# Linear attention and two MLP layers on one core: operations pinned in their queues, key maxima and scalings in fewer or other VectorE operations, one conversion unit moved

## The chip, the cores and the metric

The kernel runs on one core of a Trainium2 chip. The metric is the device time in microseconds, the median of several runs. Before the change it is 864.81 us (three runs, 862.97 to 866.43).

## The reference, cut to what matters

```python
q_s = exp(q - max(q, axis=-1)); q_s = q_s / (sum(q_s, axis=-1) + 1e-9)
k_s = exp(k - max(k, axis=2));  k_s = k_s / (sum(k_s, axis=2) + 1e-9)
kv = einsum('bhsd,bhse->bhde', k_s, v)
x = einsum('bhsd,bhde->bhse', q_s, kv)       # then heads side by side: 2304 tokens x 512
h = x @ w_in;  r = maximum(h, 0);  x = (s * r*r + b) @ w_out          # 512 -> 2048 -> 512
h = x @ w2_in; x = (h * tanh(softplus(h))) @ w2_out                   # 512 -> 2048 -> 512
```

There are 4 batches of 8 heads with 576 positions of 64. The weights of both layers arrive in float64, of which the kernel makes float32 bit by bit.

## The kernel before, in words

**Numbers.** A float32 value is held as a high part `hi`, rounded by a ScalarE copy to the type fp32r, and a low part `lo`, the VectorE subtraction `src - hi` (`split` L169, `minus` L166). A product is then three matmuls, hi by hi, hi by lo, lo by hi (`passes` L173). In chunk 0 the first nine h steps and the first seven y steps use whole float32 operands instead.

**Tiling.** The 2304 tokens are cut into five chunks, 512, 256, 512, 512 and 512 (chunks 0 to 4), and the 2048 hidden columns into 16 blocks. A *step* is one chunk and one block, so there are 80 steps; chunk c starts at step 16 c. At step n the main loop (L943) emits the y product of step n and, two steps ahead, the h product of step n + 2 with its relu and square. After step 78 the second layer begins for pairs of chunks by a seven-product scheme with operands P1 to P7 (`h_unit`, `y_pair`).

**What else runs between the products.** `at(step, kind, fn)` enters a function for a step, and `run` calls what is due; the place in the loop depends on the kind ("early", "bits", "unit", "load" and so on).

- *Weights of the first layer* (L146, L158). Pair j of weight blocks (for j = 0 w_in blocks 0 and 1, else w_in block j + 1 and w_out block j - 1) is loaded (`load_w`), converted by `bits` (a ScalarE absolute value, L129, then four VectorE operations, L130 to L141, on 128 x 1024 elements) at step j - 3, and split at step j - 2 for j of 8 and more, at step 12 + j for the others.
- *Attention of the chunks from 1 on*, a pair of heads hp at a time, in stages: `att1` (key maximum over the rows L712, transposed on TensorE and reduced; q maximum L724 and subtraction L725), `att2` (key shift L736, q exponential L740), `att3` (key exponential, q sum, reciprocal, scaling L759), `att4_mm` (kv product, q transpose), `att4`, `att5`, `att5_mm` (x). For chunk c of 2 and more, `att1` of pair hp stands at step 16 (c - 1) + 3 hp - 1, for chunk 1 at step 2 hp + 3. Chunk 0's attention runs before the loop, with its q subtraction and q scaling on POOL. `x_split` (L195) splits x two steps ahead of the next chunk.
- *Weights of the second layer*: 32 units (`unit_load`, `unit_sums`, `unit_split`): a load, `bits` on 128 x 512 elements, four sums of 128 x 128, two splits of 128 x 512, two stores from POOL's queue. STARTS (L186) gives the half step of each: three in chunk 1, 29 in chunks 2 to 4.
- *Operands of the second layer*, in chunk 4 (L0 is step 64): `b_load` reads chunks 0 and 2 back, `b_next` makes one of seven operands for each of two halves kb (`put_slot` L375), into the weight slots `w0` to `w6` as the y products of chunk 4 leave them. `ring_load` (L409) fetches second-layer weights from POOL's queue into the slots of RING (L395), first at steps L0 + 9, 11 and 13.

**What sets the order of the instructions.** Each engine executes one queue in order. A scheduler fills these queues at build time: by a model of the run, it takes an instruction when its inputs are ready, so work can stand in a queue ahead of work that the program emits earlier. `pin` (L289) ties an instruction behind all that the program has emitted before it on that engine. Pinned before the change are the relus from step U1 on, ScalarE's share of the units, and the second-layer loads on POOL.

Of the kernel before, what the change touches and what calls it, by code (L numbers as in the profile page):

```python
# [31 lines left out]
def kernel(  # L32
# [113 lines left out]
    def conv_bits(j):  # L146

        if j < WHOLE:
            t = wp.tile([P, 4 * DM], F32, tag=f"w{j}", name=f"t{j}")[:, 0:2 * DM]
        else:  # L150
            t = cv.tile([P, 2 * DM], F32, tag=f"t{j % 2}", name=f"t{j}")
        t = t.rearrange("p (z f) -> p z f", z=2)
        w_t[j] = t
        for i, (z, f) in enumerate(members(j)):
            W[z, f] = (None, t[:, i])
        bits(t, w_raw.pop(j))

# [7 lines left out]

    def minus(eng, lo, src, hi):  # L166
        eng.tensor_tensor(out=lo, in0=src, in1=hi.bitcast(F32), op=ALU.subtract)  # L167

    def split(hi, lo, src, eng=None, pin=lambda ins: None):  # L169
        pin(nc.scalar.copy(out=hi, in_=src))  # L170
        minus(eng or nc.vector, lo, src, hi)

# [11 lines left out]
    U0 = 2 * NF  # L184
    U1 = U0 - 9
    STARTS = [2 * U1, 2 * U1 + 6, 2 * U1 + 12] + [2 * U0 + 2 * (NS - 2 - U0) * e // 29 for e in range(29)]  # L186
    x_t, x_next, x_whole = {}, {}, {}
# [101 lines left out]
    def pin(ins):  # L289
        tc.keep_in_program_order(ins)  # L290
# [83 lines left out]
    def put_slot(r, kb, src):  # L374
        if kb == 0:  # L375
            x_op[r] = wp.tile([P, 2, 2, CM], F32R, tag=f"w{Y_ORDER.index(r)}", name=f"xo{r}")
        split(x_op[r][:, 0, kb], x_op[r][:, 1, kb], src)

# [13 lines left out]
    for pair in range(len(PAIRS)):  # L392
        ring += [("wi", F, i) for F in range(NU) for i in range(2)]
        ring += [("wo", r, i) for r in Y_ORDER for i in range(2)]
    RING = ("ws0", "last", "ws1")  # L395
    ring_t, ring_free, ring_done, ring_out = {}, list(RING), [], [None]
# [300 lines left out]
    def att1(b, c, hp):  # L697

        if b is not None:
# [6 lines left out]
            else:  # L706
# [4 lines left out]

            nc.vector.tensor_reduce(  # L712
                out=km.rearrange("p (h d o) -> p h d o", h=2, o=1),
                in_=kb.rearrange("p h r d -> p h d r"), axis=AX.X, op=ALU.max,
            )
            ps = att_ps(b == 0, hp % 2, f"km{b}_{hp}")
# [6 lines left out]
        mx = ap.tile([P, 2 * CM // P, 1], F32, tag="qm", name=f"qm{c}_{hp}")[:, 0:2 * rq, :]  # L723
        nc.vector.tensor_reduce(out=mx, in_=t, axis=AX.X, op=ALU.max)  # L724
        (nc.vector if c else nc.gpsimd).tensor_tensor(  # L725
# [3 lines left out]
    def att2(b, c, hp):  # L729
        if b is not None:  # L730
            kb = kv_in[b, hp][0]
            ps, km, ke = kv_mid[b, hp]
            nc.tensor.matmul(out=ps, lhsT=ones, rhs=km, start=True, stop=True)
            km = ps.rearrange("p (h d) -> p h d", h=2)
            for h in range(2):
                nc.vector.tensor_tensor(  # L736
                    out=ke[:, :, h, :], in0=kb[:, h], in1=km[:, h:h + 1, :].to_broadcast([P, RK, D]),
                    op=ALU.subtract,
                )
        nc.scalar.activation(out=q_in[c, hp], in_=q_in[c, hp], func=AF.Exp)  # L740

    def att3(b, c, hp):
# [13 lines left out]
        qn = qn[:, 0:2 * rq * D].rearrange("p (r h d) -> p r h d", r=rq, h=2)  # L756
        for h in range(2):
            o = slice(h * rq, (h + 1) * rq)
            (nc.vector if c else nc.gpsimd).tensor_tensor(  # L759
                out=qn[:, :, h, :], in0=t[:, o, :], in1=sm[:, o, :].to_broadcast([P, rq, D]), op=ALU.mult  # L760
            )
        q_in[c, hp] = qn
# [27 lines left out]

    def kv_hi(b, hp):
        hi = ap.tile([P, P], F32R, tag="kvh", bufs=NP + 1, name=f"kvh{b}_{hp}")
        lo = ap.tile([P, P], F32R, tag="kvl", bufs=NP + 1, name=f"kvl{b}_{hp}")
        kv_t[b, hp] = (hi, lo)
        nc.scalar.copy(out=hi, in_=bds[hp if b == 0 else NP])

    def kv_lo(b, hp):
        minus(nc.vector, kv_t[b, hp][1], bds[hp if b == 0 else NP], kv_t[b, hp][0])

# [64 lines left out]
    for c in range(1, NC):  # L864
        wide = CHUNKS[c - 1] == CM
        for hp in range(NP):
# [11 lines left out]
            if c == 1:  # L878
                at(hp, "att1", kv_hi, 0, hp)
                at(hp, "att1", kv_lo, 0, hp)  # L880
            at(s + o[1], "att2", att2, b, c, hp)
# [10 lines left out]
    L0 = (NC - 1) * NF  # L892
    at(U1 - 3, "load", unit_load, 0)
    for e, i in enumerate(STARTS):
# [48 lines left out]
    for n in range(NS):  # L943
# [121 lines left out]
```

## Time and profile before

| what | value |
|---|---|
| median of three runs | 864.81 us (862.97 to 866.43) |
| the profiled execution | 868.49 us |
| its span, first to last instruction | 866.7 us |
| mean granted TensorE clock | 0.988 of full speed |
| TensorE busy with matmuls | 828.4 us (96%) |
| VectorE, ScalarE, POOL busy | 616.9 us (71%), 440.8 us (51%), 109.3 us (13%) |

A matmul's busy time is modelled from its pipeline, so TensorE at 100% of a stretch says that no gap is seen, not that it runs at its peak. "Idle before" is the time an engine stood still before an instruction, and its releaser is what ended the wait. PEclk is the share of full clock that was granted.

### The profile page before, as it was taken

Reading aid. Unit: us, or ns where it says so; the run is one execution under the profiler, and the core shown is the slowest. Engines: PE = TensorE matmul, PEld = TensorE weight load, DVE = VectorE, ACT = ScalarE, POOL = GpSimd, SP = SyncE. Lnnn points to the kernel's source line nnn. Section 1 sums busy time; section 2 is a strip of 40 time slices with the busy share of each in tenths; the row PEclk is TensorE's granted clock in tenths of the full one; section 3 lists DMA queues with packets and bytes.
Section 4 is the critical chain, followed back from the end, with each engine's and each line's share of the span. In section 5 each row is a group of like instructions: output and inputs, shape, how many; then the busy total and the mean of one; then the engine's idle time right before and its main releaser. Section 6 shows DMA issues by size and latency. Waiting matters only on the chain.

```text
span 866.7 us, 11570 instructions
## 1 busy us (share of the span) xinstructions
PE 828.4 (96%) x4084; PEld 666.0 (77%) x4084; DVE 616.9 (71%) x1153; ACT 440.8 (51%) x786; POOL 109.3 (13%) x196
## 2 busy tenths in 40 slices
PE   3799999998999999999989999989999999999998
PEld 2344787987888888888868878868788888878897
DVE  6989997568888887766887448687864655786511
ACT  3645777547666666555765435255442333544322
POOL 4000000000011001120212211101111111112110
PEclk9899999998999999999999999999999999999999
DMA  6994123144666556456656889657678866687891
GB/s 170 311 376 143 27 66 112 54 103 149 207 199 205 191 196 220 165 182 216 217 186 202 272 244 374 201 189 242 220 233 281 250 177 223 217 280 262 255 375 68
DMA packets 90474, 179.02 MB, mean 207 GB/s; under 512 B 26928, under 2 KB 45104, under 8 KB 86832
## 3 DMA queue, kind: packets, MB, share of 16 engines
q0 software_dynamic: 30256, 112.73, 40.0%
q1 hardware_dynamic: 59072, 64.50, 24.2%
q10 hardware_dynamic: 1088, 1.05, 0.4%
q8 instruction: 32, 0.52, 0.3%
q14 instruction: 26, 0.21, 0.1%
HBM read 131.60 MB, written 46.66 MB: 206 GB/s over the span
## 4 chain that ended last, share of the span: by engine, by line
PE 69%; DVE 13%; DMA 11%; SPq 2%; issue 2%; ACT 2%; POOL 0%; DVEq 0%; ACTq 0%; POOLq 0%
PE P L177 22%; PE h L177 16%; PE y L177 16%; PE rh L177 3%; PE ry L177 3%; DMA q<-in_q_dram 2%; DMA raw<-in_moe_w_out_dram 2%; DVE g L348 2%; DMA kb<-in_k_dram 2%; DVE w L167 1%; DVE gly_P L167 1%; PE P3y L177 1%; PE P5y L177 1%; PE P7y L177 1%; PE P4y L177 1%
## 5 line engine op out<-in xcount | busy, mean ns | idle before, releaser
L177 PE MATMUL h<-xh,w 128*128 128x512 f32 (+1 forms) x568 | 177.6, 378 | 7.8 <-ACT r L240 4.2
L177 PE MATMUL y<-gh,w 128*128 128x512 f32 (+1 forms) x584 | 176.6, 369 | 0.0
L177 PE MATMUL P<-xoP,rw 128*128 128x512 f32 x672 | 155.2, 390 | 1.0 <-DMA rw<-wdi 1.0
L177 PEld LDWEIGHTS P<-xoP,rw 128*128 128x128 f32 x672 | 125.8, 188 | 27.3 <-issue 1.4
L177 PEld LDWEIGHTS h<-xh,w 128*128 128x128 f32 x568 | 106.2, 194 | 26.6 <-ACT r L240 4.9
L177 PEld LDWEIGHTS y<-gh,w 128*128 128x128 f32 x584 | 106.5, 188 | 17.8
L170 ACT CAST ghy_P<-g 128x512 fp32r<-128x512 f32 x112 | 69.7, 623 | 82.4 <-DVE gly_P L167 34.7
L455 DVE TENSOR_TENSOR s<-s,P 128x512 f32<-128x512 f32 x112 | 75.2, 684 | 47.7 <-PE P L177 38.3
L177 PE MATMUL h<-xl,w 128*128 128x512 f32 (+1 forms) x284 | 106.7, 376 | 0.4 <-DVE xl L167 0.4
L177 PE MATMUL y<-gl,w 128*128 128x512 f32 (+1 forms) x292 | 106.8, 369 | 0.0
L167 DVE TENSOR_TENSOR gly_P<-g,ghy_P 128x512 fp32r<-128x512 f32 x112 | 75.8, 688 | 40.1 <-ACT ghy_P L170 39.2
L177 PE MATMUL P<-ghy_P,rw 128*128 128x512 f32 x224 | 87.2, 391 | 0.0
L458 ACT ACTIVATE g<-s 128x512 f32<-128x512 f32 x64 | 39.9, 631 | 81.7 <-DVE s L455 81.4
L170 ACT CAST umem<-u 128x512 fp32r<-128x512 f32 x64 | 37.4, 619 | 51.4 <-DVE u L313 45.5
L177 PEld LDWEIGHTS h<-xl,w 128*128 128x128 f32 x284 | 55.1, 194 | 9.7 <-DVE xl L167 0.6
L177 PEld LDWEIGHTS y<-gl,w 128*128 128x128 f32 x292 | 55.0, 188 | 9.0 <-DVE gl L167 0.2
L240 ACT ACTIVATE r<-h 128x512 f32<-128x512 f32 (+1 forms) x80 | 44.0, 550 | 31.0 <-PE h L177 26.4
L167 DVE TENSOR_TENSOR gl<-r,gh 128x512 fp32r<-128x512 f32 (+1 forms) x73 | 45.7, 628 | 14.3 <-ACT gh L170 14.2
L167 DVE TENSOR_TENSOR umem<-u,umem 128x512 fp32r<-128x512 f32 x64 | 42.1, 685 | 9.9 <-ACT umem L170 9.6
L177 PEld LDWEIGHTS P<-ghy_P,rw 128*128 128x128 f32 x224 | 42.1, 188 | 8.2
L243 ACT ACTIVATE r<-r 128x512 f32<-128x512 f32 (+1 forms) x80 | 47.0, 588 | 1.9
L177 PE MATMUL P<-gly_P,rw 128*128 128x512 f32 x112 | 45.2, 404 | 2.1 <-DVE gly_P L167 1.7
(181 smaller groups left out, 1299.1 us busy)
## 6 DMA issues: line engine op xcount, KB each, us to landing
rw<-wdo POOLq DMA_DIRECT2D x28, 1024.0 KB, 5.1
wdi<-umem POOLq DMA_DIRECT2D x32, 512.0 KB, 3.6
wdo<-umem POOLq DMA_DIRECT2D x32, 512.0 KB, 4.3
rw<-wdi POOLq DMA_DIRECT2D x16, 1024.0 KB, 6.6
rw<-wdi POOLq DMA_DIRECT2D x16, 768.0 KB, 6.0
raw<-in_moe_w_in_dram SPq DMA_DIRECT2D x16, 512.0 KB, 10.0
raw<-in_moe_w_out_dram SPq DMA_DIRECT2D x16, 512.0 KB, 10.8
ur<-in_moe_w_in_dram SPq DMA_DIRECT2D x16, 512.0 KB, 4.1
```

Source lines behind the costliest of these rows:

```text
L167: eng.tensor_tensor(out=lo, in0=src, in1=hi.bitcast(F32), op=ALU.subtract)
L170: pin(nc.scalar.copy(out=hi, in_=src))
L177: mm = nc.tensor.matmul(out=ps, lhsT=x, rhs=y, start=start, stop=stop)
L240: op = nc.scalar.activation(out=r, in_=h_ps.pop(m), func=AF.Relu)
L243: nc.scalar.activation(out=r, in_=r, func=AF.Square)
L348: nc.vector.tensor_tensor(out=t.rearrange("p (a b) n -> p b a n", b=2)[:, 1], in0=t[:, 1:3], in1=t[:, 0:1].to_broadcast([P, 2, CM]), op=AL ...
L455: nc.vector.tensor_tensor(out=out, in0=a, in1=b, op=ALU.add)
L458: nc.scalar.activation(out=g[:, spot], in_=src, func=AF.Mish)
```

## The change

- `conv_bits`: the conversion of pair 0 is done in two halves of 128 x 512; the ScalarE operation of pairs from 5 on is pinned.
- `att1`: the key maximum over five rows becomes a maximum of two rows with two others (256 elements), of the two results (128), and of that with the fifth row (128), by way of a new tile `kmx`; the q maximum is pinned from chunk 1 on.
- `att2`, `att3`: the shift of the keys and the scaling of q each become one operation in place of one for each head.
- `put_slot`: ScalarE's copy is pinned; the first half's seven operands start one step later.
- chunk 0's x is split one block a step at steps with m = 5 to 8, both halves pinned, in place of all four after m = 8; the kv splits of chunk 0 are entered three steps later and pinned.
- STARTS: two units in chunk 1, 30 in the later chunks; U1 moves from step 23 to 24.
- RING begins with `last`; the first ring loads stand at L0 + 6, 10 and 14.

```diff
 conv_bits:
-        bits(t, w_raw.pop(j))
+        raw = w_raw.pop(j)
+        if j:
+            bits(t, raw, pin if j > 4 else lambda ins: None)
+        else:
+            for i in range(2):
+                bits(t[:, i], raw[:, i])
...
-    U1 = U0 - 9
-    STARTS = [2 * U1, 2 * U1 + 6, 2 * U1 + 12] + [2 * U0 + 2 * (NS - 2 - U0) * e // 29 for e in range(29)]
+    U1 = U0 - 8
+    STARTS = [2 * U1, 2 * U1 + 8] + [2 * U0 + 2 * (NS - 2 - U0) * e // 30 for e in range(30)]
...
 put_slot:
-        split(x_op[r][:, 0, kb], x_op[r][:, 1, kb], src)
+        split(x_op[r][:, 0, kb], x_op[r][:, 1, kb], src, pin=pin)
...
-    RING = ("ws0", "last", "ws1")
+    RING = ("last", "ws0", "ws1")
...
 att1:
-            nc.vector.tensor_reduce(
-                out=km.rearrange("p (h d o) -> p h d o", h=2, o=1),
-                in_=kb.rearrange("p h r d -> p h d r"), axis=AX.X, op=ALU.max,
-            )
+            rows = kb.rearrange("p h r d -> p r h d")
+            most = kmx.rearrange("p (r h d) -> p r h d", r=2, h=2)
+            kmv = km.rearrange("p (h d) -> p h d", h=2)
+            for out_, a, b_ in ((most, rows[:, 0:2], rows[:, 2:4]), (kmv, most[:, 0], most[:, 1]), (kmv, kmv, rows[:, 4])):
+                nc.vector.tensor_tensor(out=out_, in0=a, in1=b_, op=ALU.max)
...
-        nc.vector.tensor_reduce(out=mx, in_=t, axis=AX.X, op=ALU.max)
+        op = nc.vector.tensor_reduce(out=mx, in_=t, axis=AX.X, op=ALU.max)
+        if c:
+            pin(op)
 att2:
-            for h in range(2):
-                nc.vector.tensor_tensor(
-                    out=ke[:, :, h, :], in0=kb[:, h], in1=km[:, h:h + 1, :].to_broadcast([P, RK, D]),
-                    op=ALU.subtract,
-                )
+            nc.vector.tensor_tensor(
+                out=ke.rearrange("p r h d -> p h r d"), in0=kb,
+                in1=ps.rearrange("p (h o d) -> p h o d", h=2, o=1).to_broadcast([P, 2, RK, D]), op=ALU.subtract,
+            )
...
 the tables of steps:
-                at(hp, "att1", kv_hi, 0, hp)
-                at(hp, "att1", kv_lo, 0, hp)
+                at(hp + 3, "att1", kv_hi, 0, hp, pin)
+                at(hp + 3, "att1", kv_lo, 0, hp, pin)
...
-            at(L0 + 1 + 6 * kb + i, "unit", b_next, kb)
-    for s in (9, 11, 13):
+            at(L0 + 2 + 5 * kb + i, "unit", b_next, kb)
+    for s in (6, 10, 14):
         at(L0 + s, "load", ring_load)
...
 the main loop:
-            if m == H_WHOLE - 1:
-                for kk in range(NK):
-                    x_t[0, kk] = tuple(t[:, 0:CHUNKS[0]] for t in x_tiles(kk, f"0_{kk}"))
-                    split(*x_t[0, kk], x_whole[kk])
+            if H_WHOLE - 1 - NK < m < H_WHOLE:
+                kk = m - H_WHOLE + NK
+                x_t[0, kk] = tuple(t[:, 0:CHUNKS[0]] for t in x_tiles(kk, f"0_{kk}"))
+                split(*x_t[0, kk], x_whole[kk], pin, pin)
```

Left out are the new `pin` arguments of `minus`, `split`, `kv_hi` and `kv_lo`, the tile `kmx`, the one q scaling in place of two (`att3`, of the same form as `att2`), and `unit_load` of the first unit, which stays at step 20.

## Rows read from the trace of the kernel before

**Rows 1.** By stage: length, busy us (count) of PE, PEld, DVE, ACT, POOL; PEclk, DMA, GB/s
```profile
60.00:147.00 87.00, 85.70 (x403) 58.46 (x401) 78.55 (x123) 54.94 (x89) 0.21 (x2) 1.00 0.32 99
147.00:186.00 39.00, 37.58 (x313) 36.30 (x314) 23.90 (x58) 22.64 (x55) 1.09 (x11) 0.96 0.25 68
186.00:213.00 27.00, 21.22 (x186) 19.63 (x184) 19.71 (x53) 14.36 (x32) 2.12 (x6) 0.99 0.54 137
213.00:398.00 185.00, 185.00 (x897) 152.11 (x898) 142.16 (x325) 114.33 (x204) 22.95 (x39) 0.98 0.61 200
398.00:490.00 92.00, 89.16 (x387) 73.39 (x386) 74.62 (x152) 56.15 (x99) 17.50 (x24) 0.98 0.66 213
```

**Rows 2.** TensorE timeline, first products after a wait: start, us, what, [idle before <-releaser]
```profile
31.54 7.00 PE L215 MATMUL h<-x,t 128*128 128x512 f32 x12 [2.16 <-DVE t L141]
...
147.78 0.80 PE L177 MATMUL h<-xh,w 128*128 128x256 f32 x2 [0.79 <-ACT xh L170]
...
194.50 0.63 PE L788 MATMUL qt<-ident,qn 128*128 128x128 f32 x4 [1.56 <-DVE rs L807]
...
197.01 0.39 PE L177 MATMUL h<-xh,w 128*128 128x256 f32 x1 [1.40 <-ACT r L240]
...
212.83 0.79 PE L177 MATMUL h<-xh,w 128*128 128x512 f32 x1 [2.82 <-ACT xh L170]
...
441.33 0.79 PE L177 MATMUL h<-xh,w 128*128 128x512 f32 x1 [2.84 <-ACT r L240]
```

**Rows 3.** Busy time of three short stretches (columns of rows 1), for PEclk
```profile
143.00:152.00 9.00, 6.91 (x41) 6.13 (x40) 5.84 (x18) 5.57 (x15) 0.00 (x0) 0.81 0.66 200
212.00:220.00 8.00, 7.17 (x20) 5.62 (x21) 6.98 (x16) 5.54 (x12) 1.06 (x2) 0.57 0.60 204
441.00:445.00 4.00, 3.67 (x10) 2.94 (x11) 2.60 (x6) 3.25 (x7) 1.50 (x2) 0.58 0.67 234
```

**Rows 4.** VectorE timeline, 188 to 198 us
```profile
192.28 0.69 DVE L724 TENSOR_REDUCE qm<-q 128x8 f32<-128x512 f32 x1 [3.23 <-DMA q<-in_q_dram]
```

**Rows 5.** ScalarE timeline, at the end of chunk 1 and in chunk 4
```profile
194.45 0.74 ACT L745 ACTIVATE ke<-ke 128x640 f32<-128x640 f32 x1 [5.58 <-DVE rs L807]
...
209.99 0.63 ACT L740 ACTIVATE q<-q 128x512 f32<-128x512 f32 x1 [3.70 <-DVE q L725]
...
438.53 1.14 ACT L170 CAST xoP<-b 128x512 fp32r<-128x512 f32 x2 [3.62 <-PE y L177]
```

**Rows 6.** Chain that ended last: start, us, what
```profile
18.36 6.80 DMA raw<-in_moe_w_in_dram
```

**Rows 7.** Groups by line and form: busy us, mean ns | idle before, releaser
```profile
L313 DVE TENSOR_TENSOR u<-u 128x128 f32<-128x128 f32 x128 | 32.2, 285 | 1.2
...
L137 DVE SCALAR_TENSOR_TENSOR u<-ur,u 128x512 int32<-128x512 int32 x32 | 22.0, 689 | 0.5
...
L129 ACT ACTIVATE u<-ur 128x512 f32<-128x512 f32 x32 | 21.3, 667 | 13.6 <-DMA ur<-in_moe_w_out_dram 8.3 <-DMA ur<-in_moe_w_in_dram 3.4 <-DVE umem L167 1.5
...
L712 DVE TENSOR_REDUCE km<-kb 128x128 f32<-128x640 f32 x12 | 15.6, 1303 | 9.3 <-DMA kb<-in_k_dram 9.3
...
L130 DVE TENSOR_SCALAR u<-u 128x512 f32<-128x512 f32 x32 | 13.8, 433 | 23.8 <-ACT u L129 23.8
...
L736 DVE TENSOR_TENSOR ke<-kb,km 128x320 f32<-128x320 f32 x24 | 10.6, 477 | 1.9 <-PE kv L779 1.9
...
L759 DVE TENSOR_TENSOR qn<-q,qs 128x256 f32<-128x256 f32 x24 | 9.1, 418 | 2.3 <-PE x L177 2.3
...
L725 DVE TENSOR_TENSOR q<-q,qm 128x512 f32<-128x512 f32 x12 | 8.1, 674 | 0.1
...
L759 POOL TENSOR_TENSOR q<-q,qs 128x256 f32<-128x256 f32 x8 | 5.3, 678 | 6.1 <-DVE rs L807 2.6 <-DVE rs L804 1.9 <-DVE qs L751 1.6
...
L725 POOL TENSOR_TENSOR q<-q,qm 128x512 f32<-128x512 f32 x4 | 4.2, 1042 | 6.2 <-DVE qm L724 4.9 <-DMA q<-in_q_dram 1.3
...
L167 DVE TENSOR_TENSOR kvl<-bd,kvh 128x128 fp32r<-128x128 f32 x12 | 3.4, 287 | 6.0 <-ACT kvh L795 6.0
```

More of the change, by code (lines that the diff above doesn't have):

```diff
@@ L164, in conv_split, with minus, split @@
             W[z, f] = (w[:, i, 0], w[:, i, 1])
-    def minus(eng, lo, src, hi):
-        eng.tensor_tensor(out=lo, in0=src, in1=hi.bitcast(F32), op=ALU.subtract)
-    def split(hi, lo, src, eng=None, pin=lambda ins: None):
+    def minus(eng, lo, src, hi, pin=lambda ins: None):
+        pin(eng.tensor_tensor(out=lo, in0=src, in1=hi.bitcast(F32), op=ALU.subtract))
+    def split(hi, lo, src, pin=lambda ins: None, pin_lo=lambda ins: None):
         pin(nc.scalar.copy(out=hi, in_=src))
-        minus(eng or nc.vector, lo, src, hi)
+        minus(nc.vector, lo, src, hi, pin_lo)
     def passes(ps, a, b, first=True, last=True, in_order=False):
@@ L636 @@
     vb1 = ap.tile([P, RK, VW], F32, name="vb")
+    kmx = ap.tile([P, 2 * P], F32, name="kmx")
     kv_in, kv_mid, kv_ps, kv_t = {}, {}, {}, {}
@@ L733, in att2 @@
             nc.tensor.matmul(out=ps, lhsT=ones, rhs=km, start=True, stop=True)
-            km = ps.rearrange("p (h d) -> p h d", h=2)
-            for h in range(2):
-                nc.vector.tensor_tensor(
-                    out=ke[:, :, h, :], in0=kb[:, h], in1=km[:, h:h + 1, :].to_broadcast([P, RK, D]),
-                    op=ALU.subtract,
-                )
+            nc.vector.tensor_tensor(
+                out=ke.rearrange("p r h d -> p h r d"), in0=kb,
+                in1=ps.rearrange("p (h o d) -> p h o d", h=2, o=1).to_broadcast([P, 2, RK, D]), op=ALU.subtract,
+            )
         nc.scalar.activation(out=q_in[c, hp], in_=q_in[c, hp], func=AF.Exp)
@@ L756, in att3 @@
         qn = qn[:, 0:2 * rq * D].rearrange("p (r h d) -> p r h d", r=rq, h=2)
[L757 to L761, printed above, removed]
+        (nc.vector if c else nc.gpsimd).tensor_tensor(
+            out=qn.rearrange("p r h d -> p h r d"), in0=t.rearrange("p (h r) d -> p h r d", h=2),
+            in1=sm.rearrange("p (h r) o -> p h r o", h=2).to_broadcast([P, 2, rq, D]), op=ALU.mult,
+        )
         q_in[c, hp] = qn
@@ L789, in att4_mm, with kv_hi @@
         qT_ps[c, hp] = ps[:, 0:n]
-    def kv_hi(b, hp):
+    def kv_hi(b, hp, pin=lambda ins: None):
         hi = ap.tile([P, P], F32R, tag="kvh", bufs=NP + 1, name=f"kvh{b}_{hp}")
@@ L794, in kv_hi, with kv_lo @@
         kv_t[b, hp] = (hi, lo)
-        nc.scalar.copy(out=hi, in_=bds[hp if b == 0 else NP])
-    def kv_lo(b, hp):
-        minus(nc.vector, kv_t[b, hp][1], bds[hp if b == 0 else NP], kv_t[b, hp][0])
+        pin(nc.scalar.copy(out=hi, in_=bds[hp if b == 0 else NP]))
+    def kv_lo(b, hp, pin=lambda ins: None):
+        minus(nc.vector, kv_t[b, hp][1], bds[hp if b == 0 else NP], kv_t[b, hp][0], pin)
     def att4(b, c, hp):
@@ L892 @@
     L0 = (NC - 1) * NF
-    at(U1 - 3, "load", unit_load, 0)
+    at(U1 - 4, "load", unit_load, 0)
     for e, i in enumerate(STARTS):
```

## The prediction, made before the change was run

> **What bounds the kernel now.** I read the busy time by stage first [rows 1]. From 213 to 398 us TensorE is busy without a break, so nothing that lightens VectorE there can shorten the run. (Chunks are numbered 0 to 4, as in the code.) Idle TensorE time stands at three places: the turn from chunk 0 to chunk 1 (87.0 - 85.7 us up to 147, and 1.4 us after), the end of chunk 1 (27.0 - 21.22 = 5.8 us between 186 and 213), and one spot in chunk 4 (2.84 us between 398 and 490). VectorE is nearly full only in the first stage, 78.55 of 87 us. So I looked next, in TensorE's timeline, at what ended each gap [rows 2]: the first weight product waits 2.16 us for VectorE's bit conversion; the first product of chunk 1 proper waits 0.79 us for a cast; at 194.5 and 197.0 it waits 1.56 and 1.40 us; at 212.83 it waits 2.82 us for the split of x; at 441.33 it waits 2.84 us for a relu. [...]
>
> Then I asked why the releasing engines were late. At 192.28 VectorE had stood 3.23 us on a q maximum whose DMA had not landed [rows 4]. Counted in order, four maxima to a chunk, it is the first of chunk 3, whose attention is due at step 31, the last step of chunk 1. It was issued early, and everything behind it on VectorE's in-order queue waited: ScalarE's exponential sat 5.58 us behind the reciprocal that followed [rows 5], and with it a relu. At 209.99 ScalarE stood 3.70 us on the exponential of the next chunk-3 q, while the copy of x that TensorE needed was behind it. At 438.53 ScalarE stood 3.62 us on a cast into a weight slot that TensorE's y product was still reading; the relu that released TensorE was queued behind. All three are work placed too early in an in-order queue.
>
> **The change part by part.**
>
> *Q maxima pinned (chunk 1 on).* Each maximum is now issued behind all VectorE work traced before it, thus at its own step. What it newly stands behind is the key column that waits for a TensorE transpose; behind the maximum are its subtraction and the exponential one step later, and its transpose on TensorE is due four steps later, so nobody is starved. The chunk-3 work leaves the stretch 186 to 213. At stake: 1.56 + 1.40 + 2.82 = 5.8 us of gaps and 3.4 us of clock, 9.2 us. Key maxima are not pinned, and they wait for DMAs too (9.3 us over 12 [rows 7]), so I take 7.0 gained, with 0 and 9.2 as ends; what is late next there is the last pair's x and its split.
>
> *Casts of the seven operands pinned, first half one step later.* Each cast then stands behind the relu of its step, and the y product that frees its slot is two steps back instead of one. The 3.62 us wait goes, and TensorE's 2.84 us gap with its 1.7 us of clock: 4.5 at stake, 4.0 taken, ends 0 and 4.5. The first three ring loads move on POOL's queue: the slot that is free early is loaded first, at step 6 of the chunk instead of 11, the next at 10 instead of 9, and the third falls to the first second-layer unit, where its slot is free and it waits for no product. Their loads are covered by the y products still to come: 0. If that cover failed, TensorE would stand once for a load, and the chunk's 2.84 us gap is the nearest row for that. The second layer after 490 us is not touched otherwise.
>
> *One unit fewer in chunk 1.* A unit costs VectorE 2 x 0.43 + 2 x 0.69 for the bits, 4 x 0.285 for the sums and 2 x 0.67 for the splits [rows 7], 4.7 us, with its loads and its two POOL issues. It moves to stretches where VectorE is busy 142 of 185 us and 75 of 92 us [rows 1] and TensorE covers it: 0. Without that cover it would cost 4.7. In chunk 1 its going is part of the 7.0. That the relu of one step less is pinned there costs nothing either: TensorE's products order it.
>
> *Key maxima, shift, q scaling.* The key maximum took one reduce of 1.303 us; the new form is one two-operand instruction of 256 elements (0.418) and two of 128 (0.285 each), 0.99 us: 0.31 saved, 16 times. The row that decides is the reduce itself, which reads with a stride. The shift goes from 2 x 0.477 to one of 640 elements; 256 to 512 elements costs 0.256 more, so 640 costs about 0.67 + 0.13 = 0.80: 0.15 saved, 16 times. The q scaling goes from 2 x 0.418 to 0.674, 12 times; on POOL from 2 x 0.678 to 1.042 for chunk 0 [rows 7]. All this is 9 us of VectorE, but only what lies in the first stage or before a gap counts: 4 x 0.31 + 4 x 0.15 = 1.8 us of it.
>
> [...]
>
> *First conversion in halves; the splits of chunk 0's x, conversions from the sixth on and kv splits pinned or later.* The second half of the first raw tile lands at 18.36 + 6.80 = 25.2 us [rows 6]. A half takes 0.67 on ScalarE and 2 x 0.43 + 2 x 0.69 on VectorE, 2.9 us together, so it could be done by 28.1; with the key shift of the fourth pair (0.9) in between 29.0, where the product now starts at 31.54: 2.5 us earlier, between 0 (TensorE's own order holds it) and 3.4. Whether this arrives at 147 is a question of VectorE's account there. Into the stretch 60 to 147 come the four subtractions of chunk 0's x (4 x 0.67), four of kv (4 x 0.287) and the maxima, subtractions and sums of two q pairs of chunk 1 that now run before that stretch (I estimate 2 us each: four operations of 256 elements at 0.42 and small ones): 7.9 us. Out go the 1.8. Idle there is 8.45. So it just fits, and the splits of the first eight conversions, which only chunk 1 needs, may slide into 147 to 186, where VectorE has 15 us idle. The pinned conversions are due three steps before use. One new wait is likely: the last of the four splits stands behind a whole conversion (under 2 x 2.24 us by the halves) and is needed one step later. I take 0.5 gained for the whole first stage; ends: 6.3 gained (2.5, the 9.00 - 6.91 = 2.1 us idle from 143 to 152 [rows 3], and 1.7 of clock) and 8 lost (net 6.1 of work falls after the boundary, plus 1.7 of clock).
>
> **Sum.** 7.0 + 4.0 + 0.5 = 11.5 us. The profiled execution took 868.49 us (its span 866.7 and 1.8 around it), so 857.0 for such a run. It lies 3.7 above the median of 864.81, so I forecast 853.3 for the median. The smallest difference a measurement of this kernel can tell is about 0.5%, 4.3 us.
>
> **The rivals.**
> - *All of it arrives.* The first stage keeps its 2.5 us and loses no boundary: 6.3 + 9.2 + 4.5 = 20, 845. For it: the eight movable conversions. Against: VectorE's full account.
> - *The pin moves the wait instead of removing it.* Key maxima still float, and their waits for DMAs take the place of q's; half of 9.2 is left, and the new wait at the split of x costs 1.5: 4.6 + 4.0 - 1.5 = 7, about 858. This is also the case in which the pin does not do what it says.
> - *The first boundary eats the gain.* VectorE's 6.1 us fall behind it: 11 - 8 = 3, about 862, no change.
> - *Slower.* Place: steps 9 to 15 of chunk 0. The conversion of step j is now released by the relu of step j - 2 and must be split before three steps are over; if VectorE's queue makes that longer, TensorE, VectorE and ScalarE run in a loop, and TensorE stands at each step. Price: 6.1 us of work that finds no idle time, and three drops of the clock at 3.4 each, 16.3, against 11 gained: 870. It decides once the conversions take more than three steps of TensorE; for it speaks that VectorE is the fullest there, against it that a conversion needs only some 4 us of VectorE when it is alone.
>
> **How the numbers follow.** Forecast 0.47 (its own range 849 to 858), all of it 0.18, moved wait 0.15, boundary 0.13, slower 0.07. Below 860.5 lie the first three: faster 0.80, same 0.13, slower 0.07. The range 846 to 861.5 leaves out the slower case and about half of the cases at 845 and 862.
>
> **What would show it.** Right: no wait of a q maximum for its DMA between 147 and 213; TensorE busy over 25 of those 27 us and no clock below 0.9 after it; no ScalarE wait for y at a cast of the seven operands; first weight product near 29 us; key maxima in three instructions summing to 1 us. Wrong: TensorE gaps between 90 and 150 us, a longer clock drop at the start of chunk 1, key maxima with waits where q's were, or a new gap at the step after the last whole product.

## The result, and the profile after

The changed kernel took 855.74 us, the median of four runs (853.93 to 859.47), beside 865.02 (862.97 to 866.43, four runs) for the kernel before: ratio 0.990, 95% interval 0.986 to 0.994. The forecast was 853.3 with a range of 846.0 to 861.5. The profiled execution was the slowest of the four, 859.47 us with a span of 857.7. So each side's profile lies some 3.5 to 3.7 us above its own median, which matters when they are laid beside each other; four later runs of the changed kernel (e14 below) have a profile on the fast side. Over all eight runs its median is 854.7.

Of the same stages as in [rows 1, 3], in the changed kernel (length, busy us and count of PE, PEld, DVE, ACT, POOL; PEclk, DMA, GB/s):

```profile
60.00:147.00 87.00, 83.94 (x398) 58.03 (x396) 74.01 (x127) 56.12 (x94) 0.21 (x2) 1.00 0.32 96
143.00:152.00 9.00, 5.44 (x24) 4.68 (x25) 6.98 (x12) 7.47 (x17) 0.00 (x0) 0.71 0.27 96
...
186.00:213.00 27.00, 26.77 (x219) 24.76 (x218) 20.29 (x52) 17.64 (x41) 1.79 (x6) 1.00 0.52 164
398.00:490.00 92.00, 90.49 (x398) 74.32 (x397) 70.12 (x140) 53.98 (x94) 19.38 (x26) 1.00 0.65 210
```

From 186 to 213 us TensorE is now busy for 26.77 us of 27, where it was 21.22, and in chunk 4 for 90.49 of 92, where it was 89.16. At the boundary of chunks 0 and 1 it is worse: 5.44 of 9 us at a clock of 0.71, against 6.91 at 0.81. The gaps say the same. These lines of TensorE's timeline answer to [rows 2] (start, us, what, idle before and its releaser):

```profile
28.42 2.84 PE L220 MATMUL h<-x,t 128*128 128x512 f32 x6 [1.25 <-DVE t L141]
...
144.83 0.30 PE L182 MATMUL x<-qth,kvh 128*128 128x64 f32 x1 [2.04 <-ACT qth L827]
...
146.15 0.30 PE L182 MATMUL x<-qtl,kvh 128*128 128x64 f32 x1 [1.02 <-DVE qtl L172]
...
147.86 0.80 PE L182 MATMUL h<-xh,w 128*128 128x256 f32 x2 [0.68 <-ACT xh L175]
...
440.62 0.50 PE L182 MATMUL h<-xh,w 128*128 128x512 f32 x1 [0.31 <-ACT r L245]
...
458.44 1.62 PE L182 MATMUL P<-xoP,rw 128*128 128x512 f32 x6 [1.20 <-DMA rw<-wdi]
...
538.68 1.66 PE L182 MATMUL P<-xoP,rw 128*128 128x512 f32 x6 [1.68 <-DVE s L460]
...
569.38 0.50 PE L182 MATMUL P1y<-ghy_P,rw 128*128 128x512 f32 x1 [2.52 <-DVE s L460]
```

The gaps at 194.50, 197.01 and 212.83 us are gone, and the one of 2.84 us in chunk 4 is 0.31. The first weight product starts at 28.42 instead of 31.54. Three gaps at the first boundary add up to 3.7 us. New is a wait for VectorE at 538.68. The wait for a load at 458.44 is of the kind that the kernel before has further on, 0.98 us at 517.48; it comes earlier now:

```profile
517.48 2.78 PE L177 MATMUL P<-xoP,rw 128*128 128x512 f32 x11 [0.98 <-DMA rw<-wdi]
```

A running account is had by numbering TensorE's 4084 matmuls in both traces and subtracting the start of the same number before from that after (us; minus is earlier; "the account" below is this):

| near | changed kernel, profiled run | the same kernel, e14 |
|---|---|---|
| 53 us | -2.4 | -3.0 |
| 138 us | -1.4 | -2.0 |
| 160 us, behind the boundary | +1.5 | -0.3 |
| 179 us | +0.9 | -0.9 |
| 239 us, behind the end of chunk 1 | -8.9 | -10.7 |
| 427 us | -9.1 | -10.9 |
| 459 us, behind the spot in chunk 4 | -13.0 | -15.1 |
| 605 us, and from there to the end | -9.1 | -15.1 |

### The profile page after: what moved, and what is told of

The parts are those of the page before. It is cut to its first block, busy times and chain, and to the rows that moved or that the text cites. A ratio compares the mean times of both kernels' runs of the same rounds, so it can differ in the third digit from the quotient of the medians.

```text
span 857.7 us, 11568 instructions
## 1 busy us (share of the span) xinstructions
PE 827.5 (96%) x4084; PEld 665.4 (78%) x4084; DVE 615.4 (72%) x1157; ACT 439.8 (51%) x787; POOL 109.1 (13%) x192
## 4 chain that ended last, share of the span: by engine, by line
PE 57%; issue 23%; DMA 7%; DVE 6%; POOL 3%; SPq 2%; ACT 1%; POOLq 0%; DVEq 0%
PE P L182 19%; PE h L182 8%; PE y L182 8%; PE h L220 3%; PE y L263 3%; PE rh L182 3%; PE ry L182 3%; DMA xdP<-glbP 2%; POOL wdo L331 2%; DVE g L353 2%; DMA b<-yd 2%; POOL wdi L331 2%; PE P1y L182 1%; DVE gly_P L172 1%; PE P3y L182 1%
## 5 line engine op out<-in xcount | busy, mean ns | idle before, releaser
L172 DVE TENSOR_TENSOR gly_P<-g,ghy_P 128x512 fp32r<-128x512 f32 x112 | 76.0, 688 | 41.4 <-ACT ghy_P L175 39.5
L172 DVE TENSOR_TENSOR gl<-r,gh 128x512 fp32r<-128x512 f32 (+1 forms) x73 | 45.9, 629 | 18.6 <-ACT gh L175 18.2
L172 DVE TENSOR_TENSOR umem<-u,umem 128x512 fp32r<-128x512 f32 x64 | 42.3, 685 | 9.8 <-ACT umem L175 9.5
```

The costliest lines, as they stand in the source:

```text
L172: pin(eng.tensor_tensor(out=lo, in0=src, in1=hi.bitcast(F32), op=ALU.subtract))
```

## The experiments

The ratios are to the kernel before, run beside each variant on the same chip; its median was 864.5 to 864.7 us each time. Where a variant is set against the changed kernel, the median of its eight runs, 854.7 us, stands for the latter.

### Which edit emptied 186 to 213 us: e1, e2, e10, e11

**e1**, the pin alone undone:

```diff
         op = nc.vector.tensor_reduce(out=mx, in_=t, axis=AX.X, op=ALU.max)
-        if c:
-            pin(op)
```

> The changed kernel with the pin on the q maxima taken out, all else as changed. Theory: the pin is what gained the 10 us that TensorE wins between the start of chunk 1's middle and the start of chunk 2, so 863 to 866 us, with a q maximum waiting 2 to 4 us for its DMA in chunk 1 and TensorE idle 4 us or more between 186 and 213. Rival: the unit moved out of chunk 1 and the shorter key operations did it, then 856 to 859 and no such gaps.

857.0 us (856.2 to 860.45), ratio 0.991 (0.988 to 0.994), and no gap over 0.3 us from 186 to 213 us. The rival holds: with the unit moved and the operations short, the pin is not needed.

**e2**, the pin alone put into the kernel before:

```diff
-        nc.vector.tensor_reduce(out=mx, in_=t, axis=AX.X, op=ALU.max)
+        op = nc.vector.tensor_reduce(out=mx, in_=t, axis=AX.X, op=ALU.max)
+        if c:
+            pin(op)
```

> The kernel before with that pin alone added. Theory: about 9 us of the 10.5 come with it, so 855 to 858 us, TensorE busy over 26 of the 27 us from 186 to 213, and the gap near 441 us still there. Rival: the third unit in chunk 1 keeps VectorE late, then less than 4 us gained, 861 to 865.

864.46 us, ratio 0.998 (0.997 to 1.000). The gaps of [rows 2] at 194.50 and 197.01 are gone here too and that of 212.83 is down to 0.55, so for these gaps the pin by itself is nearly enough. The time of 855 to 858 us does not come with it: the account stands at -10.8 us by 376 us, and most of that is given back in chunk 4. TensorE's timeline of e2:

```profile
210.09 0.50 PE L177 MATMUL h<-xh,w 128*128 128x512 f32 x1 [0.55 <-ACT r L240]
...
390.58 0.50 PE L177 MATMUL y<-gl,w 128*128 128x512 f32 x1 [2.54 <-DVE gl L167]
...
436.09 0.79 PE L177 MATMUL h<-xh,w 128*128 128x512 f32 x1 [3.58 <-ACT r L240]
```

Behind these two gaps the account is at -3.8, and at the end at -4.2. The first is the larger loss, 4.0 us of the account with its slow clock. In VectorE's timeline its cause is a wait of the same kind as the q maximum's: a read-back of chunk 0 (`b_load`) has not landed, and the gl that TensorE needs stands behind it:

```profile
389.11 0.49 DVE L359 TENSOR_SCALAR b<-b,bsum 128x512 f32<-128x512 f32 x1 [4.20 <-DMA b<-yd]
```

In the changed kernel VectorE waits 2.74 us at this place, and TensorE has no gap there. In ScalarE's timeline the second gap of e2 is the cast of [rows 5] again, standing for y:

```profile
432.54 1.14 ACT L170 CAST xoP<-b 128x512 fp32r<-128x512 f32 x2 [3.16 <-PE y L177]
```

**e10**, the pin and the moved unit undone, the short operations kept (U1 goes back too, so the pinned relus begin one step earlier):

```diff
-    U1 = U0 - 8
-    STARTS = [2 * U1, 2 * U1 + 8] + [... * e // 30 for e in range(30)]
+    U1 = U0 - 9
+    STARTS = [2 * U1, 2 * U1 + 6, 2 * U1 + 12] + [... * e // 29 for e in range(29)]
...
-    at(U1 - 4, "load", unit_load, 0)
+    at(U1 - 3, "load", unit_load, 0)
```

and the diff of e1.

> The changed kernel with two of its parts undone together: the units of the second layer as before (three half units in chunk 1, the rest spread over 29), and no pin on the query maxima. Theory: the waits of 186 to 213 us have two causes, the floating query maximum and the third half unit of chunk 1, and the removal of either is enough; with neither removed the gaps of 5.58 and 3.70 us come back, and the time is some 7 us above the changed kernel, 861 to 865 us. Rival (the shorter key maximum, shift and scaling, still in this kernel, are the cause that counts): no gap of over 1 us there, 854 to 858 us.

862.23 us (859.27 to 864.7), ratio 0.997 (0.995 to 0.999). The time came out as the theory says, the place only in part. TensorE's timeline of e10:

```profile
209.32 0.49 PE L182 MATMUL h<-xh,w 128*128 128x512 f32 x1 [1.32 <-ACT xh L175]
...
210.24 0.49 PE L740 MATMUL km<-km,ones 128*128 128x128 f32 x2 [0.42 <-DVE km L726]
...
513.69 2.85 PE L182 MATMUL P<-xoP,rw 128*128 128x512 f32 x8 [2.61 <-DVE s L460]
```

Behind the first of them the granted clock is 0.76 from 209 to 216 us. Against e14 the account loses 3.8 us between 192 and 229 us, not the whole 9.8, and another 5.2 between 486 and 514 us, in the second layer. So "two causes" was one too few, and more than half of the 10.4 us by which its profile ends behind e14's was lost elsewhere.

**e11**, of these edits only the unit moved out: the diff of e1, the key maximum by one reduce (the diff of e6 below), and shift and scaling in halves again:

```diff
-            nc.vector.tensor_tensor(
-                out=ke.rearrange("p r h d -> p h r d"), in0=kb, ...
-            )
+            km = ps.rearrange("p (h d) -> p h d", h=2)
+            for h in range(2):
+                nc.vector.tensor_tensor(out=ke[:, :, h, :], in0=kb[:, h], ...)
...
-        (nc.vector if c else nc.gpsimd).tensor_tensor(
-            out=qn.rearrange("p r h d -> p h r d"), ...
-        )
+        for h in range(2):
+            o = slice(h * rq, (h + 1) * rq)
+            (nc.vector if c else nc.gpsimd).tensor_tensor(out=qn[:, :, h, :], in0=t[:, o, :], ...)
```

> The changed kernel with the key maximum by one tensor_reduce, the shift and the q scaling in two operations each, and no pin on the query maxima: of what the change did to chunk 1 only the move of one half unit out of it is left. Known so far: with no pin but the unit moved and the operations short, no gap over 0.3 us from 186 to 213 us; with no pin, the unit back and the operations short, gaps of 1.32 and 0.42 us and 3.4 us of slow clock; in the kernel before 5.58 and 3.70 us. Theory (load: each of unit, operations and pin takes off a part, and with the unit alone a part comes back): gaps of 1 to 5 us in sum from 186 to 213 us and 857 to 862 us. Rival (the moved unit is enough by itself): none, 853 to 856 us. Other rival (it does nothing alone): over 8 us of gaps, over 862 us.

857.07 us (854.63 to 859.42), ratio 0.991 (0.989 to 0.994). Two gaps come back, 0.67 at 193.9 and 1.37 us at 208.65, with a clock of 0.76 from 209 to 216 us as in e10; the account loses 4.3 us to e14 there. Put together, for 186 to 213 us (the kernel before and e2 lack the other edits of the change too; the two combinations that are not listed were not run):

| pin | unit moved out | short operations | gaps over 0.3 us | kernel |
|---|---|---|---|---|
| no | no | no | 5.8 | before |
| no | no | yes | 1.7 | e10 |
| no | yes | no | 2.0 | e11 |
| no | yes | yes | none | e1 |
| yes | no | no | 0.6 | e2 |
| yes | yes | yes | none | the changed kernel |

It reads as one sum of load against room: the unit and the operations each take off most of it, both together all of it, and the pin, which takes the wait for the DMA out of VectorE's queue, all but a rest by itself. That wait shrinks without the pin too: the first q maximum of chunk 3 still runs ahead of its step, at 190 to 192 us, and waits for its DMA 3.23 us in the kernel before, 1.93 in e10, 2.04 in e11 and 0.38 in e1.

### The cast in chunk 4, and the ring: e3, e4

**e3**:

```diff
-        split(x_op[r][:, 0, kb], x_op[r][:, 1, kb], src, pin=pin)
+        split(x_op[r][:, 0, kb], x_op[r][:, 1, kb], src)
```

> The changed kernel with the pin on ScalarE's casts of the seven operands taken out; they still start one step later than before the change. Theory: the pin removed ScalarE's wait for the y product, so the wait comes back with a TensorE gap of 2 to 3 us near 430 to 445 and a clock drop, 859 to 861 us. Rival: the later step alone is enough, then 855 to 857 and no gap.

862.66 us (860.5 to 864.46), ratio 0.997 (0.996 to 0.999): the pin on the cast is worth 7.9 us. (The pin without the later start was not run.) TensorE's timeline of e3, and the busy time of the stretch behind the gap (columns as above):

```profile
427.68 0.79 PE L182 MATMUL h<-xh,w 128*128 128x512 f32 x1 [5.27 <-ACT r L245]
```

```profile
428.00:432.00 4.00, 4.00 (x11) 3.12 (x11) 3.04 (x6) 2.99 (x6) 1.12 (x2) 0.58 0.75 253
```

And what ScalarE stood for ahead of that relu:

```profile
422.44 1.14 ACT L175 CAST xoP<-b 128x512 fp32r<-128x512 f32 x2 [2.91 <-PE y L182]
...
425.99 1.14 ACT L175 CAST umem<-u 128x512 fp32r<-128x512 f32 x2 [2.41 <-DVE u L318]
```

The cast waits for y as in [rows 5], and a unit's cast that got in front of the relu adds 2.41 us, so the gap is 5.27 instead of 2.84. The account loses 7.3 us to e14 at that spot; 1.6 come back by 459 us, and 2.5 more go in the second layer.

**e4**:

```diff
-    RING = ("last", "ws0", "ws1")
+    RING = ("ws0", "last", "ws1")
...
-    for s in (6, 10, 14):
+    for s in (9, 11, 13):
```

> The changed kernel with the order of the ring slots and the steps of its first three loads as before the change. Theory: the early load let one second-layer product be put 36 us ahead into chunk 4, where TensorE waits 1.2 us for the load, and the changed order cost two more in the second layer (a new wait of 1.7 us near 539 and a clock drop near 570), so 852 to 854 us, without that product at 458. Rival: the second layer's losses have another cause, then 855 to 856, only the 1.2 us wait gone.

855.95 us (854.41 to 858.4), ratio 0.988 (0.986 to 0.991): no difference that can be told, so the theory's 852 to 854 us did not come. The product that waits at 458.44 us in the changed kernel is not there; gaps of 0.82, 0.66 and 1.31 us at 474.5, 505.8 and 511.4 us stand in its place.

### The first stage: e5, e6, e7, e12, e13

**e5**, the first-stage edits undone (the bits of a slot in one call and unpinned, chunk 0's splits after the last whole h product, the kv splits three steps earlier and unpinned):

```diff
-        if j:
-            bits(t, raw, pin if j > 4 else lambda ins: None)
-        else:
-            for i in range(2):
-                bits(t[:, i], raw[:, i])
+        bits(t, raw)
...
-                at(hp + 3, "att1", kv_hi, 0, hp, pin)
-                at(hp + 3, "att1", kv_lo, 0, hp, pin)
+                at(hp, "att1", kv_hi, 0, hp)
+                at(hp, "att1", kv_lo, 0, hp)
```

> The changed kernel with the whole first-stage part undone: the bits of every weight slot in one VectorE operation and unpinned, the five splits of chunk 0's x after the last h product again, the k v splits in steps 0 to 4 and unpinned. Theory: this part is worth the head start of 2.4 us that the first h product had (28.42 against 31.54 us) and little else, and what it wins is spent at the boundary of chunks 0 and 1; so the time is that of the changed kernel within 3 us, 854 to 859 us, and the first h product is back near 31 us. Rival (the boundary's longer gaps come from the pinned bits and the moved k v splits themselves): the gaps near 146 us shrink from 3.7 us in all to about 1.9 and the slow clock there from 6.8 to 3.4 us, and the kernel is faster than the changed one, 850 to 853 us. Other rival (the pins of this part are what holds the conversions back from the path): above 861 us.

857.05 us (856.23 to 857.09), ratio 0.991 (0.989 to 0.993), by the medians 2.3 us slower than the changed kernel, though the intervals overlap. The first h product starts at 32.01 us, with a granted clock of 0.59 from 28 to 36 us, as the kernel before has 0.58 there and the changed kernel 1.00. The boundary's gaps do shrink, to 0.57 and 0.78 us, so the rival was right about the place and wrong about the time: against e14 the account is 3.9 us later at 53 us and 2.8 at 160, so the part wins more at 30 us than it loses at 146.

**e6**, the key maximum by the one reduce again:

```diff
-            for out_, a, b_ in ((most, rows[:, 0:2], rows[:, 2:4]), (kmv, ...), (kmv, kmv, rows[:, 4])):
-                nc.vector.tensor_tensor(out=out_, in0=a, in1=b_, op=ALU.max)
+            nc.vector.tensor_reduce(
+                out=km.rearrange("p (h d o) -> p h d o", h=2, o=1),
+                in_=kb.rearrange("p h r d -> p h d r"), axis=AX.X, op=ALU.max,
+            )
```

> The changed kernel with the key maxima by the one tensor_reduce again (1303 ns in chunk 1 of before, against 0.99 us for three operations). Theory: twelve of them, each 0.3 us longer, on a VectorE that is not the bound of chunks 1 to 4; the pin on the query maxima holds the rest, so 855 to 858 us and no gap of over 1 us from 186 to 213 us. Rival (the shorter key maximum is what removed the waits of 186 to 213 us, in place of the pin): with the long reduce some of the 5.58 and 3.70 us come back there, 859 to 863 us. In the first microseconds, where one operation of the three takes 0.46 to 0.62 us beside POOL, the reduce may be no slower than the three; then the first h product starts where the changed kernel has it, at 28 us.

854.26 us (850.99 to 854.62), ratio 0.987 (0.985 to 0.989). As a whole it makes no difference. Its trace, the fastest of its five runs, shows a lead in the startup: TensorE is busy for all 32.00 us from 28 to 60 (30.20 in the changed kernel), and the account is 3.9 us ahead of e14 at 53 us and 2.9 at 186. What takes this lead away in its other runs its trace does not show; e12 and e13 take the two places apart.

**e7**, the casts of the first eight weight conversions pinned as well:

```diff
-        split(w[:, :, 0], w[:, :, 1], w_t.pop(j))
+        split(w[:, :, 0], w[:, :, 1], w_t.pop(j), pin=pin if j < WHOLE else lambda ins: None)
```

> The changed kernel, and in addition the ScalarE cast of each weight that is converted from the staged whole slot (the first eight conversions, in the last steps of chunk 0 and the first of chunk 1) pinned to its step. Theory: in the changed kernel three of these casts run at 143.5, 145.8 and 148.1 us, ahead of their steps and in front of the casts for which TensorE waits at the boundary (gaps 2.04, 1.02 and 0.68 us, then 6.8 us of slow clock); pinned, they go behind those, the gaps shrink to about 1.5 us in all and the slow clock to at most 3.4 us: 850 to 853 us. Rival (the boundary waits for the chain of exponential, transposes and block-diagonal sums itself, and the casts only fill the engine while it waits): gaps as before, 854 to 858 us. Other rival (the cast, pinned to a later step, is now late for its own product): new gaps from 150 to 175 us, 858 to 862 us.

850.72 us (850.51 to 853.17), ratio 0.985 (0.982 to 0.987), 4.0 us faster than the changed kernel. ScalarE's timeline at the boundary, the changed kernel first, e7 second:

```profile
143.45 1.05 ACT L175 CAST w<-t 128x1024 fp32r<-128x1024 f32 x1
144.39 0.38 ACT L827 CAST qth<-qt 128x256 fp32r<-128x256 f32 x1
145.79 1.05 ACT L175 CAST w<-t 128x1024 fp32r<-128x1024 f32 x1 [1.02 <-DVE w L172]
```

```profile
141.22 0.38 ACT L827 CAST qth<-qt 128x256 fp32r<-128x256 f32 x1
141.47 1.08 ACT L175 CAST w<-t 128x1024 fp32r<-128x1024 f32 x1
```

The cast of qth, for which TensorE stood 2.04 us, now comes ahead of the weight's. Of the three gaps none is left (one of 0.70 us for km and one of 1.13 for gl, at 144.6 and 151.3 us, stand there), and the clock of the 24 us from 128 to 152 is 1.00 instead of 0.89.

**e12**, e7 with the reduce in chunk 0 alone:

```diff
+            if c == 0:
+                nc.vector.tensor_reduce(
+                    out=km.rearrange("p (h d o) -> p h d o", h=2, o=1),
+                    in_=kb.rearrange("p h r d -> p h d r"), axis=AX.X, op=ALU.max,
+                )
+            else:
...
```

> The kernel with the pinned weight casts (850.72 us) and the key maxima of chunk 0 alone by one tensor_reduce. Theory: in the changed kernel three VectorE operations of the startup that read two tiles of SBUF, or one in SBUF at double rate, lasted 1.0 to 1.2 us in place of 0.3 to 0.4 because a POOL operation ran beside them (5.91, 11.54, 16.97 us; an operation L726 at 12.69 us too), and no tensor_reduce did; with the reduce the key maximum takes 1.26 us whatever POOL does, the first h product starts at 27 to 28 us without the gaps of 1.25, 0.68 and 0.70 us behind it, and the time is 2 to 4 us lower, 847 to 849 us. Rival (the startup's lead is spent at the boundary of chunks 0 and 1, where the next wait stands): first h earlier, yet a gap at 140 to 150 us grows by as much, 850 to 851 us. Other rival (the startup ends with the arrival of data from DMA, whichever form is used): first h at 28.4 us as before, 850 to 851 us.

**e13**, e7 with the reduce everywhere (the diffs of e6 and e7 together):

> The kernel with the pinned weight casts and all key maxima by one tensor_reduce, as in the kernel before. Theory: in chunks 1 to 4 VectorE is not the bound and POOL hardly works, so three operations of 0.99 us in sum or one of 1.27 us make no difference: within 1 us of the run with the reduce in chunk 0 alone. Rival (at the boundary of chunks 0 and 1 and in chunk 1 the 0.3 us of each are on the path): 1 to 3 us above that run, with gaps of PE ended by qtl, xl or km on VectorE between 125 and 150 us.

e12 took 847.26 us (847.07 to 848.89), ratio 0.981 (0.979 to 0.982): 7.5 us under the changed kernel and the fastest of the study. e13 took 853.18 us (850.07 to 856.09), ratio 0.987 (0.984 to 0.989). Busy time by stretch (columns as above) of e7, e12 and e13:

```profile
28.00:60.00 32.00, 29.86 (x88) 13.21 (x89) 25.83 (x41) 15.74 (x23) 0.00 (x0) 1.00 0.99 337
...
128.00:152.00 24.00, 21.71 (x144) 18.61 (x143) 14.51 (x31) 16.39 (x35) 0.31 (x3) 1.00 0.30 91
```

```profile
28.00:60.00 32.00, 32.00 (x78) 14.29 (x77) 26.43 (x38) 15.63 (x23) 0.00 (x0) 1.00 1.00 337
...
128.00:152.00 24.00, 21.01 (x157) 18.63 (x158) 16.91 (x35) 18.23 (x37) 0.51 (x5) 1.00 0.31 92
```

```profile
28.00:60.00 32.00, 31.62 (x76) 13.96 (x75) 26.84 (x37) 15.39 (x23) 0.00 (x0) 1.00 1.00 336
...
128.00:152.00 24.00, 19.87 (x115) 16.88 (x114) 18.65 (x32) 15.24 (x31) 0.31 (x3) 0.86 0.32 98
```

With the reduce in chunk 0 the startup runs through: the first h product starts at 26.65 us, and no gap follows up to 60. A gap of 1.49 us for a weight's split stands at 148.37 us, but of the 5.3 us by which the account leads e7 at 53 us 4.6 are left at 160, so the boundary does not eat the lead. With the reduce in the other chunks too, gaps for qtl, qn and a relu (1.04, 1.17, 1.17 us) and a clock of 0.86 appear from 128 to 152 us. So the theory held for e12 and fell for e13, where the rival had the place right and the size, 1 to 3 us, too small: by the medians the reduce is 3.5 us better in chunk 0 and 5.9 worse behind it.

### The changed kernel once more: e14

> The changed kernel itself once more, beside the three others. Theory: its profiled execution (859.47 us) was the slowest of its four, and the 1.68 us gap at 538.7 us and the 3.4 us of slow clock at 570 us, which no other run of this study with these units shows, belong to that execution alone: the median is again 854 to 857 us and the profiled execution has no gap of over 1 us from 520 to 560 us. Rival: they are there again, so the second layer of this kernel does lose them each time and the experiments won them.

853.97 us (853.08 to 855.21), ratio 0.988 (0.986 to 0.990). From 490 to 545 us TensorE was busy for 53.03 us in the first profile; in this one:

```profile
490.00:545.00 55.00, 55.00 (x243) 45.04 (x242) 41.41 (x64) 25.79 (x43) 8.45 (x12) 1.00 0.95 309
```

The gap at 538.68 us is in one of the two traced executions of this kernel, so the change alone does not make it: there VectorE had stood 1.8 us for DMAs (xdP<-glbP). The gap at 569.4, 2.52 us in the first profile, is 1.75 in this one, about the 2.02 of before. Of the kernel before only one execution was traced, so where its 3.7 us above the median lie stays open, and with it some of the 15.1 us in the account of e14; the medians give 10.

## Why the prediction was right, and where it was not

*Q maxima pinned, 7.0 of 9.2.* Measured 9.8 us in the account, in either profile: 2.8 more than the term, and 0.6 above its upper end. Of the signs named, no q maximum waits for its DMA between 147 and 213 us, TensorE is busy for over 25 of 27 us, and the clock stays at 1.00. The mechanism is right, and the pin alone does gain some 9 us there (e2). What failed is the sentence that gives the edit this gain and adds of the unit only that "its going is part of the 7.0": e1 gains some 9 us there without the pin. The change removed these gaps twice over, by the pin (all but 0.55 us) and by the unit and the short operations together. Nor does the gain of the pin last by itself: in e2 chunk 4 gives most of it back, which the prediction's sum of separate terms has no place for. The clock terms are [rows 3], a stretch's length times the share of the clock that was not granted: 8 x 0.43 = 3.4 us here, 9 x 0.19 and 4 x 0.42 = 1.7 us at the boundary and in chunk 4; in that trace the granted clock is 0.50 from 212.3 to 219.1 us, from 147.4 to 150.8 and from 441.0 to 444.4, which gives the same. The rival by which key maxima take over the wait did not come: they still wait (8.3 us over 12, against 9.3 [rows 7]), but no gap of TensorE follows from 186 to 213 us.

*Casts pinned, 4.0 of 4.5.* The account moves by 3.9 to 4.3 us at the spot, and among what the casts of these operands stand for there is no y product any more. Right. Its value to the whole is larger, 7.9 us by e3: without the pin the gap is not the old 2.84 us but 5.27 (e3) or 3.58 (e2), so part of what chunk 1 gains is lost here. How much of the edit is the later start was not tried.

*Ring and unit at 0.* e4 agrees for the ring. Where the unit went to, TensorE stays busy (185.00 of 185 us from 213 to 398 in the changed kernel, as before).

*First stage, 0.5.* Measured +0.3 in e14 and -1.5 us in the first profile, so right in size, but by luck, as a sum of parts that were each misjudged. The 2.5 us at the first product came as 2.4 to 3.0, and a part of them is a clock that the prediction did not read: from 28 to 36 us it is 0.58 before and 1.00 after (the kernel before first, the changed kernel second):

```profile
28.00:36.00 8.00, 5.84 (x28) 3.25 (x28) 6.98 (x12) 3.53 (x7) 0.00 (x0) 0.58 0.96 245
```

```profile
28.00:36.00 8.00, 6.90 (x34) 3.10 (x35) 6.18 (x12) 2.43 (x5) 0.00 (x0) 1.00 0.80 208
```

By e5 the stage's own edits are worth 2.3 us, and the new form of chunk 0's key maxima, which the term counted as a gain, costs 3.5 (e12 beside e7). Then the boundary took it back, as the rival "the first boundary eats the gain" has it, with 2.9 us in the first profile where the rival has 8, and for another reason: not VectorE's account, which is lighter (74.01 of 87 us instead of 78.55), but ScalarE's order. The sentence that failed is that the splits of the first eight conversions "may slide" behind 147 us. They were free to float and slid forward, in front of the casts that TensorE waited for; e7 holds them back and wins 4.0 us. Two of the signs of being wrong thus came, TensorE gaps between 90 and 150 us and a longer drop of the clock at the start of chunk 1 (0.71 over the 9 us where it was 0.81; e14 has the gaps, with 0.81).

*Prices of the VectorE operations.* Groups by line and form of the changed kernel (busy us, mean ns, idle before and its releaser):

```profile
L743 DVE TENSOR_TENSOR ke<-kb,km 128x640 f32<-128x640 f32 x12 | 9.8, 817 | 2.8 <-PE kv L785 2.7
...
L722 DVE TENSOR_TENSOR kmx<-kb 128x256 f32<-128x256 f32 x12 | 5.1, 422 | 8.3 <-DMA kb<-in_k_dram 8.3
...
L722 DVE TENSOR_TENSOR km<-kmx 128x128 f32<-128x128 f32 x12 | 3.4, 286 | 0.2
L722 DVE TENSOR_TENSOR km<-km,kb 128x128 f32<-128x128 f32 x12 | 3.4, 285 | 0.2
...
L722 DVE TENSOR_TENSOR kmx<-kvb 128x256 f32<-128x256 f32 x4 | 2.5, 616 | 2.5 <-DMA kvb<-in_k_dram 2.5
...
L722 DVE TENSOR_TENSOR q<-kmx 128x128 f32<-128x128 f32 x4 | 1.9, 482 | 0.0
L726 DVE TENSOR_SCALAR q<-ident,q 128x128 f32<-128x128 f32 x4 | 1.9, 474 | 0.0
L722 DVE TENSOR_TENSOR q<-q,kvb 128x128 f32<-128x128 f32 x4 | 1.8, 462 | 0.3 <-DMA kvb<-in_k_dram 0.3
```

Twelve key maxima take 0.422 + 0.286 + 0.285 = 0.99 us and the shift 0.817, as forecast (0.99, 0.80). The four of the startup, the very ones whose saving was counted, take 0.616 + 0.482 + 0.462 = 1.56 us, and the L726 behind each 0.474. In the kernel before:

```profile
L712 DVE TENSOR_REDUCE q<-kvb 128x128 f32<-128x640 f32 x4 | 5.0, 1256 | 1.4 <-DMA kvb<-in_k_dram 1.4
...
L719 DVE TENSOR_SCALAR q<-ident,q 128x128 f32<-128x128 f32 x4 | 1.1, 280 | 0.0
```

So "4 x 0.31" saved was 4 x 0.30 = 1.2 us lost: the prices came from rows of the later chunks, and were carried to a place where another engine works beside VectorE (in the changed kernel POOL is busy for 11.49 of the first 28 us and for 0.21 of the 87 from 60 to 147). The 0.19 us more of L726 are one long operation of 1.06 us among the four, and cannot be put down to the form of the key maximum: with the reduce its mean is 0.480 us in e12 and 0.304 in e6. The reduce itself held: 1.260 us in e12, beside 1.256 in the kernel before.

*The median.* 853.3 was forecast, 855.74 measured, 854.7 over eight runs. The terms come to 11.5 us, the medians to 10, and the accounts of the two profiles to 9.1 and 15.1. In them the end of chunk 1 gives 2.8 us more than its term, the first stage 0.2 to 2.0 less, and the second layer takes 3.9 in one and nothing in the other; that the sum came out so near is in part luck.

## What to carry to other kernels

A stall at the end of a full stage can be a sum of load against room: several edits may each remove most of it (here 5.8 us of gaps became 1.7 in e10, 2.0 in e11 and 0.6 in e2), and only taking them away one by one, and then two at a time, says which are needed. Work that nobody waits for yet must be held back on an in-order queue on every engine that issues it; pinning it on one engine leaves it free to get in the way on the next (with the q maxima pinned on VectorE, the free weight casts on ScalarE still cost 4.0 us, e7). And the price of an operation holds for the stretch where it was read: look at what the other engines do there before carrying it over (the three operations of a key maximum took 0.99 us in the later chunks and 1.56 in the startup). A gain in one stage is also not yet a gain of the run: e2 led by 10.8 us and kept 4.2, because early work of VectorE and ScalarE in the next stage stood waiting for its inputs (4.20 us for a read-back, 3.16 for a y product).

## What was not expected of the hardware

In the startup four VectorE operations lasted 1.01 to 1.22 us beside GpSimd's, where others of their form take 0.28 to 0.42, and a reduce beside one kept its 0.67. The timeline of the startup of the changed kernel, VectorE first, GpSimd (POOL) second:

```profile
5.91 1.01 DVE L722 TENSOR_TENSOR q<-q,kvb 128x128 f32<-128x128 f32 x1 [0.32 <-DMA kvb<-in_k_dram]
...
11.54 1.22 DVE L722 TENSOR_TENSOR kmx<-kvb 128x256 f32<-128x256 f32 x1
12.69 1.06 DVE L726 TENSOR_SCALAR q<-ident,q 128x128 f32<-128x128 f32 x1
...
14.73 0.67 DVE L756 TENSOR_REDUCE qs<-q 128x8 f32<-128x512 f32 x1
...
16.97 1.08 DVE L722 TENSOR_TENSOR q<-kmx 128x128 f32<-128x128 f32 x1
```

```profile
5.74 1.04 POOL L734 TENSOR_TENSOR q<-q,qm 128x512 f32<-128x512 f32 x1 [1.54 <-DVE qm L731]
...
11.44 1.04 POOL L734 TENSOR_TENSOR q<-q,qm 128x512 f32<-128x512 f32 x1 [1.35 <-DVE qm L731]
12.44 1.22 POOL L764 TENSOR_TENSOR q<-q,qs 128x512 f32<-128x512 f32 x1
14.62 1.04 POOL L734 TENSOR_TENSOR q<-q,qm 128x512 f32<-128x512 f32 x1 [0.96 <-DVE qm L731]
16.85 1.04 POOL L764 TENSOR_TENSOR q<-q,qs 128x512 f32<-128x512 f32 x1 [1.19 <-ACT q L747]
```

Each of the four long VectorE operations (0.28 to 0.42 us when alone) starts 0.10 to 0.25 us behind a GpSimd operation and ends 0.09 to 0.28 us behind its end. The reduce at 14.73 starts 0.11 us behind one and takes its usual 0.67. In the other direction the GpSimd operation at 12.44, started while a VectorE maximum was still open, takes 1.22 instead of 1.04. Of the four that lasted long, three are a tensor_tensor and one is the tensor_scalar L726; the tensor_tensor L743 at 9.68, which also began beside a GpSimd operation (9.05 to 10.09), took its usual 0.81. (The "double rate" in e12's theory is that of a tensor_scalar: for 128 x 1024 elements L130 takes 0.688 us where the tensor_tensor L172 takes 1.223, for 128 x 512 0.427 and 0.686.) Why these four end only behind the GpSimd operation and the reduce and L743 do not, no run shows. Nor was it tried by itself whether these long operations alone make e7 slower than e12 (the startup with GpSimd's work elsewhere); e12 changes the operation, and its L726, now L732, still takes 0.480 us in the mean of four, where it is 0.280 in the kernel before.
